# Layer 0 transposed on TensorE for all chunks, and another order of the weight loads, in a four-layer attention and feed-forward kernel

## The chip, the core and the metric

The kernel runs on one core of a Trainium2 chip. The metric is the device time of one execution in microseconds (us); lower is better. Times of runs are given with their median. The profile is that of one execution. Its names for the engines are PE (TensorE), PEld (TensorE's loads of the stationary operand), DVE (VectorE), ACT (ScalarE), POOL (GpSimd) and SP (SyncE, which here issues DMAs only). DMAs are issued on two queues, that of SP and that of ACT, and are carried out by 16 DMA engines.

## The reference

Four residual layers follow one another on x of 2048 rows (tokens) by 448 columns, in bf16: attention, feed-forward, attention, feed-forward. Both attention layers use the same weights, and so do both feed-forward layers.

```python
def _A_ref(x, wqkv, wo):                 # H = 16 heads of Dh = 28, window W = 8, dilation 2
    q, k, v = ...                        # x @ wqkv, split into heads
    idx = pos[:, None] - off[None, :]    # off = 0, 2, ..., 14; only idx >= 0 counts
    logits = jnp.einsum("bhsd,bhswd->bhsw", q, kg) * scale
    attn = _softmax(logits, axis=-1)
    o = jnp.einsum("bhsw,bhswd->bhsd", attn, vg)
    return o... @ wo

def _B_ref(x, w_gate, w_up, w_down):     # F = 1792
    h = (x @ w_gate) * (x @ w_up)
    return h @ w_down

x = x + _A_ref(_layernorm(x), A_wqkv, A_wo)
x = x + _B_ref(_layernorm(x), B_w_gate, B_w_up, B_w_down)
x = x + _A_ref(_layernorm(x), A_wqkv, A_wo)
x = x + _B_ref(_layernorm(x), B_w_gate, B_w_up, B_w_down)
```

## The kernel before

**Tiling.** Even tokens and odd tokens are put into the two halves of a 2048-column order, so that a dilated window becomes a window of 8 neighbours. Everything is cut along the tokens: 16 blocks of 128 for the normalisation, chunks of 256 or 512 (`ACH`, `BCH`, line 56) for the projections, and 17 query blocks of 120 or 128 for the attention. A job such as A03 is chunk 3 of layer 0, B10 is chunk 0 of layer 1. `SEQ` (line 65) lists the 19 jobs. All of x stays in SBUF (`x_sb`), and all weights are loaded once.

**A job of attention.** `ln_chunk` (line 570) normalises each block: statistics on DVE (line 580), the inverse root on ACT (lines 583 and 585), the normalised block `xn_sb` on DVE (line 601). The block then has to be transposed into `xnTa`. `PE_T` (line 28) lists the chunks for which TensorE does it: four transposes into one bank of PSUM (line 610), and one copy to `xnTa` on ACT or DVE (line 616). All other blocks go through one DMA transpose each, issued by SP (line 604). Layer 0 has the chunks 00 to 04 with 2, 4, 4, 4 and 2 blocks. `qk_chunk` (line 668) multiplies with the query and key weights (matmuls recorded at line 648), and ACT or DVE copies the result to `qk` (line 700). The last 4 heads' values of most query blocks take another path: their weights are packed into unused columns of the query/key projection (line 531), SP writes these rows of the result to a tensor `vt` in HBM (line 709), and a DMA transpose brings them back as columns of `v2_sb` (line 720; the profile calls the destination `v_sb`). The rows of ones that go with them are written to `vt` by SP once (line 540). Then follow the scores (line 791), the exponential (ACT, line 798), the mask (DVE or POOL, line 804), the product with the values (line 824; with ones at line 818 for the first four query blocks), the division, and the product with `wo` (line 664), which is added to `x_sb` (line 876).

**A job of feed-forward.** The normalised block is transposed by DMA into `xnTb`. Fourteen units of 14 matmuls (line 905) make gate and up from `WGU`, whose partitions 0 to 63 hold the gate weights and 64 to 127 the up weights. ACT copies the gate (line 911), DVE multiplies (line 914). The result times `WD` (lines 664 and 926) is added to `x_sb`.

**What sets the order.** A planner in the file (`Sched`, line 112) fixes the order of all instructions on each engine before the program is built. It simulates the engines with an assumed duration for each operation and an assumed latency (`lat`) for each DMA, and at each step lets a free engine take the ready operation with the lowest priority number. For TensorE it also weighs changes of the matmul's tile mode (`HOLD_A`, `HOLD_BA`, `HOLD_BB`). Priorities come from the job's place in `SEQ`, a table by job (`JP`), one by kind of operation (`PR`), and for layer 0's normalisation `HEAD_P`. On the chip each engine runs its list in order and waits on semaphores where an operation needs another's result. A wrong assumption thus leaves the order in place and turns into a wait.

**The loads around the change.** SP issues x, part of the query/key/value weights, `wo` (line 544), and the up weights (line 545) without any wait but for the memset of `wo_g`. ACT issues the gate weights (line 546) when the first key projection is complete, and the down weights in two halves (line 548) when the first eight blocks are normalised and the first part of chunk 01's projection is copied out. `BL` (line 53) holds the assumed latencies of gate, up and down weights.

Of the kernel before, what the change touches and what calls it, by code (L numbers as in the profile page):

```python
# [24 lines left out]
ACT_TABLE_SET = 6  # L25

MAIN = "R64"
PE_T = ('00', '01', '02')
HEAD_LN = 5
HEAD_P = (-38.93, -34.69, -18.9, -18.15, -15.19)  # L30
HOLD_A = 0.0
HOLD_BA = 2000.0
HOLD_BB = 2000.0
HOLD_N = 3
D_PE = 1
# [9 lines left out]
AVC = True  # L45
AVC_E = ("act", "dve")
NBK = 8
PR = {'E': 5.39, 'lnv': 4.48, 'N': 2.54, 'S': 1.51, 'H': -16.8, 'VT': 0.06, 'QK': 1.71, 'G': -2.51, 'R': -2.54, 'Tps': 24.4, 'Ddps': -3.29, 'V': 4.0, 'Yps': -16.04, 'rstd': -2.61, 'Rs': -4.21, 'Rl': -7.93, 'mv': -22.02, 'Ex': 2.02, 'Oc': 6.51, 'QKps': -1.79, 'x': -0.68, 'Gps': 21.63, 'PW': -1.17, 'bn': 1.13, 'xn': 0.26, 'T': -5.31, 'AV': 2.17, 'VVps': -0.71}
JP = {'A04': 17.51, 'B32': 73.91, 'B33': -39.49, 'A00': -57.97, 'B12': -8.89, 'A22': 3.6, 'B10': -7.69, 'B14': -6.07, 'B13': -6.69, 'A21': -6.5, 'B11': 5.61, 'B31': 5.7, 'B34': -23.55, 'A01': -1.05, 'A23': -9.97, 'A02': -0.45, 'A20': -23.59, 'B30': 0.59, 'A03': -0.27}
XL = (3000.0, 3000.0, 4500.0, 5000.0, 5500.0)  # L50
WVL = 5000.0
STL = (3300.0, 4300.0, 3500.0, 4600.0)
BL = (9000.0, 13000.0, 11000.0)
WOL = 6000.0
PLAIN = 4
ACH = {0: (256, 512, 512, 512, 256), 2: (512, 512, 512, 512)}
BCH = {1: (256, 512, 512, 512, 256), 3: (256, 512, 512, 512, 256)}
WARM = 18
FILL = 30
SEED = 459  # L60
JITTER = 0
ATT_P = 0.26
A_CAP = 5
B_CAP = 8
SEQ = "A00 A01 B10 A02 B11 A03 A04 B12 A20 B13 A21 B14 B30 A22 B31 A23 B32 B33 B34".split()
# [28 lines left out]

class Op:
    __slots__ = ("engs", "ins", "est", "deps", "mode", "prio", "acquire", "release", "idx", "eng",
                 "dma", "lat", "after", "start", "end", "seen", "selfd")

    def __init__(self, **kw):
        for k in self.__slots__:  # L100
# [11 lines left out]
class Sched:  # L112
# [10 lines left out]
        self.ready = {}  # L123
        self.rng = random.Random(SEED)

    def add(self, engs, ins, est, deps=(), prio=0.0, mode=None, acquire=None, release=(), dma=None, lat=0.0, after=None, selfd=()):
        if isinstance(engs, str):
            engs = (engs,)
        if not isinstance(est, dict):
            est = {e: float(est) for e in engs}  # L130
        op = Op(engs=engs, ins=ins, est=est, deps=[d for d in deps if d is not None], mode=mode, prio=prio,
                acquire=acquire, release=release, idx=len(self.ops), dma=dma, lat=lat, after=after, selfd=set(selfd))
        op.deps += list(selfd)
        op.prio += JITTER * self.rng.random()
        for _, k in ins:
            k = k[0] if isinstance(k, list) and k else k
            if isinstance(k, tuple) and k[0] in PR and k[0] != "cross":
                op.prio += PR[k[0]]
                break
        self.ops.append(op)  # L140
        for n, (fn, keys) in enumerate(ins):
            for k in (keys if isinstance(keys, list) else [keys]):
                if k is not None:
                    assert k not in self.ready, k
                    self.ready[k] = (op, n)
        return op
# [11 lines left out]
    def ready_at(self, op, eng):  # L158
        r = 0.0
        for k in op.deps:  # L160
            f = self.finish_of(k)
            if f is None:
                return None
            src = self.ready[k][0]
            if src.dma is not None:
                lat = 60.0
            elif src.eng == eng:
                lat = (self.SELF_LAT if k in op.selfd else 0.0) if eng == "pe" else self.SAME + self.TAIL[eng]
            else:
                lat = self.PE_LAT if src.eng == "pe" else self.LAT + self.TAIL[src.eng]  # L170
            r = max(r, f + lat)
        if op.after is not None:
            if op.after.end is None:
                return None
            r = max(r, op.after.end)
        return r
# [18 lines left out]
    def schedule(self):  # L195
# [27 lines left out]
        while left:  # L223
            moved = False
            b_ready = any(o.acquire is not None and o.acquire.kind == 1 for o in pend["pe"])
            for e in self.ENGS:
# [54 lines left out]
                if op.acquire is not None:  # L281
                    op.acquire.b = self.pick_banks(op.acquire, now)
                    for b in op.acquire.b:
                        self.holder[b] = op.acquire
                        if self.last_rel[b] is not None:
                            op.deps.append(self.last_rel[b])
                est = op.est[e]
                if e == "pe":
                    if mode is not None and op.mode != mode:
# [115 lines left out]
def build(nc, A_x, A_wqkv, A_wo, B_w_gate, B_w_up, B_w_down, out):  # L405
# [41 lines left out]
    sc = Sched()  # L447
    LAST = sc
    sem_names = ["pe", "act", "dve", "pool"]
    sem_names += [f"d_x{i}" for i in range(NCH)] + ["d_stg0", "d_stg1", "d_stg2", "d_stg3", "d_wv", "d_wo", "d_wg", "d_wu", "d_wd0", "d_wd1", "d_out", "d_out2"]  # L450
    sem_names += ["d_x0h"]
    sem_names += [f"d_t{li}_{j}" for li in range(4) for j in range(len(CH[li]))]
    sem_names += [f"d_p{li}_{j}" for li in (0, 2) for j in range(len(CH[li]))] + [f"d_v{q}" for q in range(NQB)] + ["d_one0", "d_one2", "d_stv"]
# [6 lines left out]
        atl = mybir.InstLoadActFuncSet(name=nc.get_next_instruction_name(), ins=[], outs=[], act_func_set_id=ACT_TABLE_SET)  # L460
        return E.add_instruction(atl)

    def plain_dma(q, dst, src, key, sem, deps=(), lat=3000.0, prio=0.0):
        sc.add(q, one(lambda E: E.dma_start(dst, src), key), {"sp": 520.0, "act": 500.0, "pool": 1000.0}[q], deps=deps, dma=sem, mode=0, lat=lat, prio=prio)  # L464

    CH_ROWS = [0, 128, 192, 320]
    stage = hT[:].rearrange("p f s n -> p (f s n)")
# [69 lines left out]
    sc.add("pool", one(lambda E: E.memset(big1, 1.0), "c_big1"), 1800, prio=-20)  # L537
    for li in (0, 2):
        dst = vt_dram[li].rearrange("(t r) n -> t r n", r=32)[:, DH:32, :]
        plain_dma("sp", dst, big1, ("vones", li), f"d_one{li}", deps=["c_big1"], lat=3000.0, prio=-30)  # L540
    for j in range(4):
        dst = wo_g[32 * j:32 * j + DH, :, :]
        src = A_wo.rearrange("(c j e) d -> j e c d", c=4, j=4, e=DH)[j]
        plain_dma("sp", dst, src, ("wo", j), "d_wo", deps=["c_wo"], lat=WOL, prio=-45)
    plain_dma("sp", WGU[64:128, :, :], B_w_up.rearrange("(k p) f -> p k f", p=64), "wu", "d_wu", lat=BL[1], prio=-44)
    plain_dma("act", WGU[0:64, :, :], B_w_gate.rearrange("(k p) f -> p k f", p=64), "wg", "d_wg", lat=BL[0], deps=[("Kps", 0, 0, 0)], prio=-90)
    for n in range(2):
        plain_dma("act", WD[:, 7 * n:7 * n + 7, :], B_w_down[F // 2 * n:F // 2 * n + F // 2, :].rearrange("(c p) e -> p c e", p=128), ("wd", n), f"d_wd{n}", deps=[("rstd", 0, 7), ("QK", 0, 1, 0)], lat=BL[2], prio=-19)
    WDR = [("wd", 0), ("wd", 1)]
    WO = [("wo", j) for j in range(4)]  # L550

# [18 lines left out]
    def ln_chunk(li, j, prio):  # L570
# [17 lines left out]
        for B in blocks:  # L588
# [13 lines left out]
                   325.0 if par == 0 else 540.0, deps=[("rstd", li, B), ("mv", li, B), ("x", li - 1, B), prev], prio=prio - 0.2)  # L602
            if not by_pe:
                sc.add("sp", one(lambda E, slot=slot, c0=c0: E.dma_start_transpose(X[:, :, c0:c0 + 128], xn_sb[:, slot, 0:128 * nt]), ("T", li, B)),
                       1300.0, deps=[("xn", li, B)] + war, dma=f"d_t{li}_{j}", mode=0, lat=3000.0 if li == 0 else 1400.0 if par == 0 else 1900.0, prio=prio)
            else:
                bk = Banks(1)
                ins = []
                for c in range(4):
                    ins.append((lambda E, c=c, slot=slot, bk=bk: E.transpose(ps[:, bk[0], :].bitcast(bf)[:, 128 * c:128 * (c + 1)], xn_sb[:, slot, 128 * c:128 * (c + 1)], ident[:]),  # L610
                                ("Tps", li, B) if c == 3 else None))
                sc.add("pe", ins, 4 * 56.0, deps=[("xn", li, B), "c_id"], mode="F", acquire=bk, prio=prio)
                def ft(E, c0=c0, bk=bk):
                    src = ps[:, bk[0], :].bitcast(bf)[:, 0:512].rearrange("p (c n) -> p c n", c=4)
                    dst = X[:, :, c0:c0 + 128]
                    return E.activation(dst, src, ACT.Copy) if hasattr(E, "activation") else E.tensor_copy(dst, src)
                sc.add(("act", "dve"), one(ft, ("T", li, B)), {"act": act_est(512), "dve": dve_est(512)}, deps=[("Tps", li, B)] + war, release=[(bk, 0)], prio=prio)
# [50 lines left out]
    def qk_chunk(li, j, prio):  # L668
# [37 lines left out]
        for b, w in [(b, w) for b in range(4) for w in range(2) if b + w < 4 and (li, j) != (0, 0)]:  # L706
            src = qk[32 * b + DH:32 * b + 32, w, :, c0:c1]
            dst = vt_dram[li].rearrange("(t w b r) n -> r w b t n", w=2, b=4, r=4)[:, w, b, :, c0:c1]
            sc.add("sp", one(lambda E, dst=dst, src=src: E.dma_start(dst, src), ("PW", li, j) if b == 3 else None), 550.0, deps=[("QK", li, j, c) for c in range(4)], dma=f"d_p{li}_{j}", mode=0, lat=3500.0 if li == 0 and j <= 2 else 2200.0, prio=prio - 0.2)

    vslot, v2slot = {}, {}

    def vt_load(li, qb, prio):
# [3 lines left out]
        slot, prev = ring("v2", ("AV", li, qb))  # L717
        v2slot[(li, qb)] = slot
        deps = [("PW", li, j) for j in chunks_of(li, k0, k0 + nk)] + [("vones", li), prev]
        sc.add("sp", one(lambda E: E.dma_start_transpose(v2_sb[:, slot, :], vt_dram[li][:, k0:k0 + 128]), ("VT", li, qb)), 1300.0, deps=deps, dma=f"d_v{qb}", mode=li, lat=2500.0 if li == 0 and k0 < 1024 else 1500.0, prio=prio)  # L720

    def v_group(li, qbs, prio):
        X = xnT[0]
# [161 lines left out]
    def b_chunk(li, j, n_b, prio):  # L885
# [7 lines left out]
        def unit(fc):  # L893
            acq = Banks(2, kind=1)
            def out(which):
                return ps[:, acq[which], 0:nt]
            return dict(bk=acq, out=out, n=nt, deps=["wg", "wu"],
                        keys=(("Gps", li, j, fc), ("Ups", li, j, fc)), fc=fc)

        us = [unit(fc) for fc in range(FC)]  # L900
# [158 lines left out]
```

## Time and profile before

Thirteen runs took 398.99 to 405.2 us, with a median of 404.39 us.

| | value |
|---|---|
| profiled execution, device time | 404.39 us |
| its span, from the first to the last instruction | 402.7 us |
| matmuls | 5046 |
| HBM read / written | 8.54 MB / 2.83 MB |
| transposes by TensorE (line 610) | 40, from 7.6 to 19.6 us |
| DMA transposes into `xnTa` in layer 0 (line 604) | 6, issued from 25.1 to 38.2 us |
| first feed-forward matmul (line 905) | 59.78 us |
| last matmul (line 926) begins a group at | 394.77 us |

A row of the views by engine reads: line, engine, operation, output tile <- input tiles, the shape, the number of instructions behind an x. What stands in brackets is idle time of that engine before the row, and what ended it. In the timeline a row begins with its start and its length in us, and neighbours of one kind are merged. In the page's 40 slices one digit stands for a fortieth of the span, about 10 us, and gives the busy share in tenths. In a view of windows a row gives the stretch, its length, and for PE, PEld, DVE, ACT and POOL the busy us and the number of instructions, then the granted TensorE clock as a share of the full one, the share of the DMA engines' time and GB/s. A view of waits gives the waiting engine and line, what ended the wait, the sum in us, how often, and the longest.

### The profile page before, as it was taken

To read this page: it belongs to the slowest core of one execution; us is meant where nothing else is said; L and a number is where in the kernel's file an instruction comes from. 1 tells how busy PE (TensorE), PEld (TensorE's weight loads), DVE (VectorE), ACT (ScalarE), POOL (GpSimd) and SP (SyncE) were. 2 spreads that over 40 slices of the span, in tenths; PEclk is the share of its full clock that TensorE was granted. 3 is DMA by queue.
4 is the path that set the end of the run, shared out by engine and by line. 5 is a ranking of instruction groups with operands and counts; after the bars stand their busy time and mean duration, and the time that the engine had idled before them with its cause. 6 is when DMAs were issued, how large, how long until landed. Compare 5 with 4: busy or idle time off the path is not lost.

```text
span 402.7 us, 11719 instructions
## 1 busy us (share of the span) xinstructions
PE 387.9 (96%) x5046; PEld 210.5 (52%) x5046; DVE 293.3 (73%) x603; ACT 223.4 (55%) x406; POOL 15.4 (4%) x28
## 2 busy tenths in 40 slices
PE   8994999999999999999999999999999999999996
PEld 5541457644454444545455676744445455444584
DVE  5986498989997988688688955936684777674152
ACT  5874487666753945565564565624661575343040
POOL 6223000000000000000000000000000000000000
PEclk9998799999999999999999999999999999999999
DMA  8999141325025112222020205031030300320010
GB/s 267 239 240 197 25 61 27 62 54 67 12 47 73 29 30 45 47 28 39 15 40 10 54 13 105 18 60 43 11 47 24 70 0 3 91 48 2 13 36 24
DMA packets 57171, 23.34 MB, mean 58 GB/s; under 512 B 48064, under 2 KB 56192, under 8 KB 57120
## 3 DMA queue, kind: packets, MB, share of 16 engines
q1 hardware_dynamic: 54400, 18.86, 24.4%
q10 hardware_dynamic: 2720, 3.73, 3.9%
q8 instruction: 40, 0.66, 0.6%
q14 instruction: 11, 0.09, 0.1%
HBM read 8.54 MB, written 2.83 MB: 28 GB/s over the span
## 4 chain that ended last, share of the span: by engine, by line
PE 86%; DVE 4%; DMA 4%; ACT 3%; issue 1%; SPq 0%; DVEq 0%
PE ps L905 42%; PE ps L664 26%; PE ps L648 13%; DMA xnTa<-xn_sb 3%; PE ps L824 2%; PE ps L791 2%; DMA x_sb<-in_A_x_dram 1%; ACT E_sb L798 1%; PE ps L926 1%; DVE E_sb L804 1%; ACT qk L700 1%; DVE x_sb L876 1%; DVE xn_sb L601 0%; SPq L464 0%; DVE qk L700 0%
## 5 line engine op out<-in xcount | busy, mean ns | idle before, releaser
L905 PE MATMUL ps<-xnTb,WGU 64*128 64x512 bf16 (+1 forms) x1960 | 179.3, 333 | 2.2 <-DVE R_sb L840 0.8
L905 PEld LDWEIGHTS ps<-xnTb,WGU 64*128 64x128 bf16 x1960 | 96.3, 94 | 73.7 <-issue 2.2
L911 ACT ACTIVATE g_sb<-ps 128x512 bf16<-128x512 f32 (+1 forms) x140 | 71.4, 512 | 89.1 <-PE ps L905 88.0
L914 DVE TENSOR_TENSOR hT<-g_sb,ps 128x512 bf16<-128x512 bf16 (+1 forms) x140 | 78.9, 573 | 45.3 <-ACT g_sb L911 42.5
L664 PE MATMUL ps<-WD,hT 64*128 64x448 bf16 x840 | 85.3, 349 | 0.2
L798 ACT ACTIVATE E_sb<-ps 128x960 bf16<-128x960 f32 (+1 forms) x68 | 62.6, 972 | 11.2 <-PE ps L791 11.1
L648 PE MATMUL ps<-xnTa,WQK 64*128 64x512 bf16 (+1 forms) x504 | 55.2, 360 | 6.6 <-DMA xnTa<-xn_sb 6.0
L664 PEld LDWEIGHTS ps<-WD,hT 64*128 64x128 bf16 x840 | 39.8, 94 | 37.1 <-PE ps L664 1.1
L876 DVE TENSOR_TENSOR x_sb<-x_sb,ps 128x448 bf16<-128x448 bf16 x62 | 35.9, 613 | 16.0 <-PE ps L664 15.7
L804 DVE TENSOR_TENSOR E_sb<-E_sb,MK 128x960 bf16<-128x960 bf16 (+1 forms) x64 | 43.8, 699 | 4.5 <-ACT E_sb L798 4.5
L580 DVE BATCH_NORM_STATS2 st<-x_sb 128x6 f32<-128x448 bf16 x64 | 37.4, 613 | 3.0 <-DMA x_sb<-in_A_x_dram 3.0
L648 PEld LDWEIGHTS ps<-xnTa,WQK 64*128 64x128 bf16 x504 | 23.4, 95 | 30.6 <-issue 8.3
L601 DVE TENSOR_SCALAR xn_sb<-x_sb,mv,rstd 128x512 bf16<-128x512 bf16 (+1 forms) x64 | 34.3, 569 | 1.0 <-ACT rstd L585 0.8
L664 PE MATMUL ps<-wo_g,oT 64*128 64x448 bf16 x256 | 29.6, 350 | 0.0
L700 ACT ACTIVATE qk<-ps 128x1024 bf16<-128x1024 f32 (+1 forms) x22 | 19.7, 906 | 17.1 <-PE ps L648 17.1
L700 DVE CAST qk<-ps 128x1024 bf16<-128x1024 f32 (+1 forms) x14 | 16.0, 1142 | 12.0 <-PE ps L648 12.0
L842 ACT ACTIVATE R_sb<-R_sb 128x480 f32<-128x480 f32 (+1 forms) x30 | 18.0, 603 | 10.4 <-DVE R_sb L840 10.2
L648 PE MATMUL ps<-WV,xnTa 64*128 64x336 bf16 (+2 forms) x252 | 22.8, 301 | 0.1
L858 DVE TENSOR_TENSOR oT<-O_sb,R_sb 128x480 bf16<-128x480 f32 (+3 forms) x32 | 19.5, 614 | 2.6 <-ACT R_sb L844 2.5
L844 ACT ACTIVATE R_sb<-R_sb 128x480 f32<-128x480 f32 (+1 forms) x34 | 20.3, 602 | 0.6
L840 DVE STREAM_SHUFFLE R_sb<-O_sb 128x480 f32<-128x480 f32 (+1 forms) x30 | 20.5, 689 | 0.0
L583 ACT ACTIVATE lnv<-mv,eps_sb 128x2 f32<-128x2 f32 (+1 forms) x33 | 9.7, 293 | 18.1 <-DVE mv L582 17.9
(55 smaller groups left out, 179.4 us busy)
## 6 DMA issues: line engine op xcount, KB each, us to landing
out_dram<-x_sb SPq DMA_DIRECT2D x15, 112.0 KB, 1.7
WGU<-in_B_w_up_dram SPq DMA_DIRECT2D x1, 1568.0 KB, 17.6
WGU<-in_B_w_gate_dram ACTq DMA_DIRECT2D x1, 1568.0 KB, 20.3
WD<-in_B_w_down_dram ACTq DMA_DIRECT2D x2, 784.0 KB, 15.9
x_sb<-in_A_x_dram SPq DMA_DIRECT2D x3, 448.0 KB, 5.8
vt<-qk SPq DMA_DIRECT2D x49, 16.0 KB
xnTb<-xn_sb SPq DMA_TRANSPOSE x32, 3.0
v_sb<-vt SPq DMA_TRANSPOSE x30, 2.7
```

The source lines that it names most:

```text
L580: sc.add("dve", one(lambda E, B=B: E.bn_stats(st6[:, B, :], x_sb[:, B, :]), ("bn", li, B)), 525.0, deps=[("x", li - 1, B)] + ([("xn", li - ...
L601: sc.add("dve", one(lambda E, B=B, dst=dst, src=src: E.tensor_scalar(dst, src, mv[:, B, 0:1], rstd[:, B:B + 1], ALU.subtract, ALU.mult), ( ...
L648: parts[0 if s < 3 else 1][1].append((lambda E, w=w, c=c, lo=lo, st=st, sp_=sp_: E.matmul(u["out"](w), u["lhs"](w, c, lo, lo + 64), u["rhs ...
L664: ins.append((lambda E, w=w, c=c, lo=lo, st=st, sp_=sp_: E.matmul(outs(w), lhs(w, c, lo), rhs(w, c, lo), start=st, stop=sp_), keys[w] if s ...
L700: return E.activation(dst, src, ACT.Copy) if hasattr(E, "activation") else E.tensor_copy(dst, src)
L798: return E.activation(E_sb[0:nk, slot, 2 * hp:2 * hp + 2, 0:4 * nq], ps[0:nk, b0:b0 + 2, 0:4 * nq], ACT.Exp, scale=SCALE)
L804: return E.tensor_tensor(e, e, m, ALU.mult)
L840: sc.add("dve", one(lambda E: E.stream_shuffle(R_sb[:, rs, 0:4 * nq], osrc(), [DH] * 32), ("Rs", li, qb)), dve_est(4 * nq) + 100.0, deps=[ ...
L876: sc.add("dve", one(lambda E: E.tensor_tensor(x_sb[:, B, :], x_sb[:, B, :], ps[:, bk[w], 0:D], ALU.add), ("x", li, B)), dve_est(D), deps=[ ...
L905: ins.append((lambda E, u=u, k=k, w=w: E.matmul(u["out"](w), WGU[64 * w:64 * w + 64, k, 128 * u["fc"]:128 * u["fc"] + 128], X[64 * w:64 * ...
L911: sc.add("act", one(lambda E, gs=gs, bk=bk: E.activation(g_sb[:, gs, 0:nt], ps[:, bk[0], 0:nt], ACT.Copy), ("G", li, j, fc)), act_est(nt), ...
L914: sc.add("dve", one(lambda E, gs=gs, bk=bk, fc=fc: E.tensor_tensor(hT[:, fc, hs, 0:nt], g_sb[:, gs, 0:nt], ps[:, bk[1], 0:nt], ALU.mult), ...
```

## The change

All five chunks of layer 0 are transposed on TensorE. The down weights are issued by SP, before the up weights, without a wait. The gate weights (ACT) and the up weights (SP) are each cut into two pieces, of 3 and 4 of the 7 parts of `WGU`, each with a semaphore of its own, and the feed-forward matmuls wait for all four. In place of its wait, a gate piece gets an earliest time in the planner's own simulation (`tmin`, from `KT`: 13.0 and 13.5 us). The planner adds a dependency for such an operation if SP issues it. The rows of ones for `vt` get a later priority. The assumed latencies change, and so do all priority tables, one hold time, the number `ATT_P` and the seed.

```diff
-PE_T = ('00', '01', '02')
+PE_T = ("00", "01", "02", "03", "04")
-HEAD_P = (-38.93, -34.69, -18.9, -18.15, -15.19)
-HOLD_A = 0.0
-HOLD_BA = 2000.0
+HEAD_P = (-41.16, -25.35, -17.52, -19.02, -16.79)
+HOLD_A = 2000.0
+HOLD_BA = 4000.0
...
-BL = (9000.0, 13000.0, 11000.0)
+BL = (11000.0, 15000.0, 8000.0)
+KP = ((0, 3), (3, 7))
+KT = (13000.0, 13500.0)
...
-ATT_P = 0.26
+ATT_P = -0.3
...
+        if op.tmin is not None:
+            r = max(r, op.tmin)
...
+                if op.tmin is not None and e == "sp":
+                    gate = [o for o in order["pe"] if o.end + self.PE_LAT <= now and isinstance(o.ins[-1][1], tuple) and o.ins[-1][1] in self.ready]
+                    op.deps.append(gate[-1].ins[-1][1])
...
-        plain_dma("sp", dst, big1, ("vones", li), f"d_one{li}", deps=["c_big1"], lat=3000.0, prio=-30)
+        plain_dma("sp", dst, big1, ("vones", li), f"d_one{li}", deps=["c_big1"], lat=3000.0, prio=-10)
...
-    plain_dma("sp", WGU[64:128, :, :], B_w_up.rearrange("(k p) f -> p k f", p=64), "wu", "d_wu", lat=BL[1], prio=-44)
-    plain_dma("act", WGU[0:64, :, :], B_w_gate.rearrange("(k p) f -> p k f", p=64), "wg", "d_wg", lat=BL[0], deps=[("Kps", 0, 0, 0)], prio=-90)
+    for n, (k0, k1) in enumerate(KP):
+        plain_dma("sp", WGU[64:128, k0:k1, :], B_w_up[64 * k0:64 * k1, :].rearrange("(k p) f -> p k f", p=64), ("wu", n), f"d_wu{n}", lat=BL[1], prio=-43.5)
+        plain_dma("act", WGU[0:64, k0:k1, :], B_w_gate[64 * k0:64 * k1, :].rearrange("(k p) f -> p k f", p=64), ("wg", n), f"d_wg{n}", lat=BL[0], tmin=KT[n], prio=-90)
     for n in range(2):
-        plain_dma("act", WD[...], ..., ("wd", n), f"d_wd{n}", deps=[("rstd", 0, 7), ("QK", 0, 1, 0)], lat=BL[2], prio=-19)
+        plain_dma("sp", WD[...], ..., ("wd", n), f"d_wd{n}", lat=BL[2], prio=-44)
...
-            return dict(bk=acq, out=out, n=nt, deps=["wg", "wu"],
+            return dict(bk=acq, out=out, n=nt, deps=[(w, n) for w in ("wg", "wu") for n in range(2)],
```

Also changed, in numbers only: the tables `PR` and `JP`, `SEED`, and three more assumed DMA latencies (layer 0's transposes, writes of `vt` and transposes back).

## The prediction

> **What bounds the kernel now.** I read the page first, for the shares and the 40 slices:
>
> ```profile
> PE 387.9 (96%) x5046; PEld 210.5 (52%) x5046; DVE 293.3 (73%) x603; ACT 223.4 (55%) x406; POOL 15.4 (4%) x28
> PE   8994999999999999999999999999999999999996
> PEclk9998799999999999999999999999999999999999
> DMA  8999141325025112222020205031030300320010
> ```
>
> TensorE is busy for 387.9 of 402.7 us, so 14.8 us are all that a better order can win without shortening its work. Two slices stand out, the fourth and fifth (10 us each, 30 to 50 us): there the busy digit is 4 and the granted clock dips. Next I asked what TensorE itself waited for, longest first:
>
> ```profile
> PE ps L648 <- DMA xnTa<-xn_sb: 6.0, 1, 6.0
> PE ps L515 <- DVE eps_sb L493: 1.1, 1, 1.1
> PE ps L926 <- DVE hT L914: 0.9, 1, 0.9
> PE ps L905 <- DVE R_sb L840: 0.8, 1, 0.8
> ```
>
> One wait holds 6 of the 14.8 us: a query/key projection waits for a normalised block that the DMA transposes. Nothing else passes 1.1 us, and from 60 to 390 us the idle time sums to 1.7 us (from windows of 40, 100, 100 and 90 us). The timeline of TensorE and of the SP queue shows the place:
>
> ```profile
> 32.92 1.69 PE L648 MATMUL ps<-xnTa,WQK 64*128 64x512 bf16 x14
> 40.65 1.46 PE L648 MATMUL ps<-xnTa,WQK 64*128 64x512 bf16 x6 [6.04 <-DMA xnTa<-xn_sb]
> 42.04 0.59 PE L818 MATMUL ps<-E_sb,ones 128*32 128x480 bf16 x4
> ...
> 25.11 6.95 SPq L604 DMA_TRANSPOSE xnTa<-xn_sb  x4
> 32.11 3.02 SPq L709 DMA_DIRECT2D vt<-qk  x7
> 35.17 4.36 SPq L604 DMA_TRANSPOSE xnTa<-xn_sb  x2
> ```
>
> The four transposes of chunk 03 are issued from 25.11 us; the last lands at 40.5 us. The chain of waits agrees: it contains one piece of 10.62 us, from 29.90 us, for such a transfer. Layer 0's six transposes land a median 9.5 us after issue, layer 2's sixteen 2.5 us. The difference is the traffic beside them: the gate and up weights (1568 KB each, issued at 11.38 and 10.25 us, landing 20.3 and 17.6 us later), then the two halves of the down weights (issued at 21.46 and 22.09 us, 14.7 to 17.1 us to land). The plan in the kernel priced the transposes at 3.0 us, so its order of TensorE is 6.5 us too optimistic there: that is the stall.
>
> The windows show what the stall costs afterwards:
>
> ```profile
> 34.60:40.65 6.05, 0.01 (x3) 0.03 (x1) 2.85 (x3) 0.27 (x1) 1.99 (x1) 0.80 1.19 140
> 40.65:45.80 5.15, 5.15 (x42) 1.72 (x42) 0.66 (x1) 2.05 (x3) 0.00 (x0) 0.57 0.06 10
> 45.80:50.00 4.20, 4.20 (x64) 2.30 (x62) 3.40 (x5) 2.05 (x4) 0.00 (x0) 1.00 0.12 23
> ```
>
> The seventh value is the granted clock (0.57 for 5.15 us after the stall), the eighth the DMA share.
>
> **What the Trainium skill says.** "TensorE: Matmul & The Clock Gate", Part 1: an idle window of about 3.4 us drops TensorE to half its clock, and about 3.4 us of work bring it back. The trace agrees (0.57 on average for 5.15 us, then 1.00). Part 4 of that page prices a 128x128 TensorE transpose at about 275 ns in a kernel, output to PSUM, so with a copy after it. Here one lasts 219 ns, but they overlap: four cost less than half of four durations. "DMA: Bandwidth & Descriptors", Queues, rings and completion order: each DMA engine consumes one issuer's ring in order and alternates between issuers by packet. So SP's transposes shared the engines with ACT's weights, which the 9.5 us against 2.5 fit; it also says that what SP issues behind big weights on its own queue starts behind them. No wait of this trace isolates that.
>
> **The change part by part.**
>
> 1. *The stall goes*: the six DMA transposes of chunks 03 and 04 become TensorE transposes. −6.04 us of idle time.
>
> 2. *The clock after it*: between 40.65 and 45.80 us TensorE did 22 projections of 512 columns (6 + 16), one set of 4 ones-matmuls and one of 16 value products. At full clock 28 such projections took 3.12 us (21.56 to 24.68 us), so 22 take 2.45; the two sets took 0.56 (21.00 to 21.56 us). 3.01 us against 5.15: −2.14 us. If a shorter stall of over 3.4 us stays, this part stays too.
>
> 3. *Transposes on TensorE*: 6 blocks x 4 = 24. Starts in the timeline: eight take 0.55 us (13.67 to 14.22), four 0.33 us (14.77 to 15.10), so 69 to 83 ns each: 1.7 to 2.0 us on the engine that bounds. I take +2.0.
>
> 4. *Their copies out of PSUM*: 6 more, of 0.60 us on ACT or 0.39 on DVE, 2.4 to 3.6 us in all. From 25 to 35 us ACT is busy 8.80 of 10 us, DVE 7.61: 3.6 us free together, a thin cover; from 34.6 to 50 us both are half empty. I take 0, upper bound 3.6. A bank of PSUM is held for each; same bound. A gain here is excluded, it is added work.
>
> 5. *Queues.* SP loses six transpose issues (6.95 + 4.36 = 11.3 us of its time) and gains the two halves of the down weights and one more up piece, three at 0.39 to 0.76 us: +1.2 to 2.3 us near 10 us. Behind these on SP stand the constant rows of `vt` (11.06 us now), which move back too by their own priority, then the `vt<-qk` writes, the transposes into `v_sb`/`v2_sb`, and those into xnTb. First `vt<-qk` today waits until 32.11 us, behind the transposes, though its last input is copied out at 27.34 us; it can now be issued some 4.8 us earlier. ACT loses two issues (0.77 us at 21.5 us) and gains one of 0.39 to 0.69 us near 13 us. The 13.0/13.5 us release is used only by the planner: its extra dependency is written for SP, and the gate pieces are issued by ACT, so no wait is added. Sum on the path: 0, between −0.5 and +0.5.
>
> 6. *When the weights land.* Ahead of them come x (1.84 MB), wqkv (1.2) and wo (0.4). By 10 us 2.67 MB are moved (182 and 351 GB/s for 5 us each); the remaining 0.8 MB and 3 x 1.61 MB at the 243 GB/s of 10 to 35 us need 23 us: all is in at about 33 us, at the 209 GB/s of the slowest window at 37 us. The gate and up weights, last instead of first, come 2 to 5 us later than their 31.7 us; their first user starts at 59.78 us, 8 us earlier if the stall goes: 51.6 us. The cover is 15 us. The down weights are used at 76.6 us. Cost 0.
>
> 7. *New priorities everywhere, another tie order*: the order of all engines is planned anew. Between 60 and 390 us at most 1.7 us of idle can be won, some 1.8 more at the start of the second chunk and the end (0.84 + 0.93). It can also lose: I bound it by −2.5 and +4 (twice as much idle again as that part and the two small waits have). I take 0.
>
> Sum: −6.04 − 2.14 + 2.0 = −6.2 us against the profiled execution, 404.39 us with a span of 402.7. That execution equals the median of the 13 runs. **398.2 us.** The fastest run of the kernel before, 398.99 us, is near what remains if the stall is almost absent, which fits.
>
> **The rivals.**
>
> *The wait moves (part of the gain is kept or none).* Without the stall ACT and DVE must do the work of 25 to 50 us in 17; the copies of point 4 (3.6) or a worse order (4) come onto the path: 398.2 + 3.6 to 398.2 + 7.6, 402 to 406. For it: ACT and DVE are 88% and 76% busy there. Against it: through the stall they idle, so the work left over is small.
>
> *The values come late: slower than before.* Value products from the fifth query block on need columns that go out by `vt<-qk` and return transposed, all on SP. On SP's queue the down and up weights are now ahead of them. By point 6 these end at 33 to 37 us; the writes take 2 us more, the transpose 1.3 to issue and 2.7 to land: 39 to 43 us. Today the fifth product stands at 57.45 us, moved up by 8.2 it is at 49 us, and there is no wait. It decides if the new order puts that product before about 40 us. The fourth block's scores are at 32.60 us, so 33 us is the earliest that I can argue: 10 us of wait to 43 and 2.1 us for the clock, 398.2 + 12.1 = 410.3 us. Gate and up weights used before 33 to 37 us would do the same, but the first feed-forward chunk needs attention output, normalisation and transposes first, 13.5 us today (46.33 to 59.78).
>
> *The change doesn't do what it says.* If the pipeline of copies had bounded 35 to 50 us anyway, removing the DMA wait would bring nothing and the transposes cost 2: 406.4 us. Against it: ACT was idle 7.8 us before its next step in the stall, DVE 6.5 us.
>
> **How the numbers follow.** A measurement of this kernel can tell about 1% from no change: 400.35 and 408.43 us are the limits. The stall goes and nothing takes its place: 0.64, 395 to 400.3. The wait moves, or nothing is won: 0.22, 400.4 to 408. Late values, late weights or a clearly worse order: 0.14, over 408.4. The low end is 398.2 − 2.5 (point 7) − 0.3 (point 3) − 0.5 (point 5), about 394.9, with 0.4 for a run's own spread: 394.5. The high end, 406.0, takes in the first rival's bound (405.8); about 0.06 lies below, and 0.14 above. Faster 0.64, same 0.22, slower 0.14.
>
> **What would show it.** Right: no wait of TensorE for xnTa in layer 0, a granted clock of 1.00 from 5 us on, 64 TensorE transposes instead of 40, first feed-forward product near 52 us. Point 4 wrong: TensorE waits for ACT or DVE copies between 15 and 50 us. Point 5 or 6 wrong: a wait of TensorE for `v_sb<-vt`, WGU or WD. Point 7 wrong: more than 3 us of idle between 60 and 390 us. The forecast falls if a wait over 3.4 us, with the clock after it, stands anywhere else.

## The result, and the profile after

The kernel after takes **399.75 us** (median of 11 runs, 398.79 to 400.33); beside it the kernel before takes 404.06 us (48 runs, 398.99 to 405.7). The ratio is 0.9915, with a 95% interval of 0.9887 to 0.9943. The ratio leaves out runs of a kernel that are more than 1.5% above its fastest, ten of the 48 of the kernel before, so it stands nearer to 1 than the quotient of the medians (0.9893). The forecast was 398.2 us within 394.5 to 406. The profiled execution took 398.79 us with a span of 397.1, against 404.39 and 402.7: 5.6 us less. It is the fastest of the 11 runs, and the profiled execution before lies at the median of its own, so the traces show a larger gain than the 4.3 us between the medians.

The page of the kernel after, shares and slices:

```profile
PE 386.9 (97%) x5070; PEld 212.7 (54%) x5070; DVE 289.6 (73%) x599; ACT 227.2 (57%) x413; POOL 16.2 (4%) x31
PE   8988999999999999999999999999999999999996
PEclk9999999999999999999999999999999999999999
DMA  8992142412212310221120224203103020320000
```

The hole in the fourth slice and the dip of the clock in the fourth and fifth are gone, and the DMA engines are full for three slices, not four. But the third and fourth slice show an 8 for TensorE. The waits of TensorE in the kernel after, longest first:

```profile
PE ps L522 <- DVE eps_sb L500: 1.1, 1, 1.1
PE ps L934 <- DVE hT L922: 0.9, 1, 0.9
PE ps L656 <- DVE oT L866: 0.8, 1, 0.8
PE ps L913 <- DMA xnTb<-xn_sb: 0.8, 1, 0.8
PE ps L618 <- DVE qk L708: 0.7, 1, 0.7
PE ps L656 <- ACT WQK L530: 0.5, 1, 0.5
PE ps L826 <- DVE E_sb L812: 0.5, 1, 0.5
PE ps L618 <- DVE xn_sb L609: 0.5, 1, 0.5
```

(Line numbers are 7 or 8 higher than before.) No wait for a transposed block of layer 0 is left. In its place stand four short ones for VectorE between 22 and 35 us, 0.7 + 0.5 + 0.5 + 0.8 = 2.5 us.

The books by stretch, from windows of TensorE's busy time, before and after:

```profile
0.00:60.00 60.00, 50.30 (x675) 27.50 (x677) 43.69 (x95) 39.76 (x72) 15.35 (x28) 0.94 0.81 173
0.00:60.00 60.00, 54.99 (x778) 32.96 (x780) 49.15 (x108) 45.47 (x86) 16.24 (x31) 1.00 0.65 164
```

From 0 to 60 us it idled 9.70 us before and 5.01 us after, so 4.7 us are won there. From 60 to 380 us it is 1.74 against 1.83 us, no change. Busy time over the whole span fell by 1.0 us although 24 transposes were added, because work at a lower clock counts as busy for longer.

### The profile page after: what moved, and what is told of

Same layout as the page of the kernel before. It is cut to its first block, busy times and chain, and to the rows that moved or that the text cites. A ratio compares the mean times of both kernels' runs of the same rounds, so it can differ in the third digit from the quotient of the medians.

```text
span 397.1 us, 11796 instructions
## 1 busy us (share of the span) xinstructions
PE 386.9 (97%) x5070; PEld 212.7 (54%) x5070; DVE 289.6 (73%) x599; ACT 227.2 (57%) x413; POOL 16.2 (4%) x31
## 3 DMA queue, kind: packets, MB, share of 16 engines
q10 hardware_dynamic: 912, 2.12, 2.0%
## 4 chain that ended last, share of the span: by engine, by line
PE 84%; DVE 9%; DMA 3%; SPq 1%; issue 1%; ACT 1%; DVEq 0%
PE ps L913 42%; PE ps L672 25%; PE ps L656 12%; PE ps L799 2%; PE ps L832 2%; DVE xn_sb L609 2%; DVE st L588 2%; DMA x_sb<-in_A_x_dram 2%; DVE E_sb L812 2%; PE ps L934 1%; SPq L471 1%; DMA xnTb<-xn_sb 1%; DVE qk L708 1%; DVE x_sb L884 1%; DVE hT L922 0%
## 5 line engine op out<-in xcount | busy, mean ns | idle before, releaser
L656 PE MATMUL ps<-xnTa,WQK 64*128 64x512 bf16 (+1 forms) x504 | 53.0, 353 | 0.8 <-ACT WQK L530 0.5
L812 DVE TENSOR_TENSOR E_sb<-E_sb,MK 128x960 bf16<-128x960 bf16 (+1 forms) x64 | 42.6, 673 | 4.2 <-ACT E_sb L806 4.2
L609 DVE TENSOR_SCALAR xn_sb<-x_sb,mv,rstd 128x512 bf16<-128x512 bf16 (+1 forms) x64 | 36.2, 601 | 1.3 <-ACT rstd L593 1.2
L708 ACT ACTIVATE qk<-ps 128x1024 bf16<-128x1024 f32 (+1 forms) x28 | 25.2, 916 | 14.2 <-PE ps L656 13.9
L672 PEld LDWEIGHTS ps<-wo_g,oT 64*128 64x128 bf16 x256 | 12.4, 94 | 11.4 <-DVE x_sb L884 0.3
L656 PEld LDWEIGHTS ps<-WV,xnTa 64*128 64x128 bf16 x252 | 11.6, 94 | 10.5 <-ACT R_sb L852 1.2
## 6 DMA issues: line engine op xcount, KB each, us to landing
WGU<-in_B_w_up_dram SPq DMA_DIRECT2D x1, 896.0 KB, 19.2
```

The source lines that it names most:

```text
L609: sc.add("dve", one(lambda E, B=B, dst=dst, src=src: E.tensor_scalar(dst, src, mv[:, B, 0:1], rstd[:, B:B + 1], ALU.subtract, ALU.mult), ( ...
L656: parts[0 if s < 3 else 1][1].append((lambda E, w=w, c=c, lo=lo, st=st, sp_=sp_: E.matmul(u["out"](w), u["lhs"](w, c, lo, lo + 64), u["rhs ...
L672: ins.append((lambda E, w=w, c=c, lo=lo, st=st, sp_=sp_: E.matmul(outs(w), lhs(w, c, lo), rhs(w, c, lo), start=st, stop=sp_), keys[w] if s ...
L812: return E.tensor_tensor(e, e, m, ALU.mult)
```

## The experiments

All variants but one keep the planned order of every engine (*frozen*): the plan is made as usual, and the lists are edited after `sc.schedule()`. So a part of the change can be done or undone without a new plan. The runs fall into three groups on three chips. The kernel before ran beside each group, and its median moved between 402.34 and 403.29 us, so differences of half a microsecond between groups say little. The second number under "runs" counts those whose granted clock, averaged over the whole run, lies below 1.00.

| run | what it is | runs, below 1.00 | median us | before beside it | ratio, 95% interval |
|---|---|---|---|---|---|
| b_weights | before, only the weight loads changed | 6, 6 | 405.87 | 402.34 | 1.0102 [1.0063, 1.0141] |
| b_fill | before, the wait filled with idle matmuls | 20, 0 | 400.88 | 402.34 | 0.9979 [0.9958, 1.0001] |
| a_oldw | after, weight loads of before | 20, 0 | 400.29 | 402.34 | 0.9953 [0.9937, 0.9969] |
| a_look | after, unchanged | 4, 0 | 399.73 | 403.29 | 0.9897 [0.9861, 0.9933] |
| a_dma6 | after, six DMA transposes again | 5, 2 | 400.01 | 403.29 | 0.9903 [0.9870, 0.9936] |
| a_dma6l | the same, issued later | 5, 4 | 400.29 | 403.29 | 0.9916 [0.9886, 0.9947] |
| a_dma2 | the same, chunk 04 alone | 4, 0 | 399.78 | 403.29 | 0.9901 [0.9866, 0.9936] |
| a_dma6o | after, both structural parts undone | 20, 11 | 400.34 | 402.54 | 0.9969 [0.9945, 0.9992] |
| b_pet | before, TensorE transposes, planned anew | 4, 3 | 407.93 | 402.54 | 1.0151 [1.0082, 1.0219] |
| a_nopool | after, POOL's four masks on VectorE | 12, 0 | 398.54 | 402.54 | 0.9910 [0.9878, 0.9941] |
| a_npd | a_nopool with a_dma6l | 4, 0 | 397.62 | 402.54 | 0.9897 [0.9822, 0.9971] |

**The kernel before, once more (b_look).** No edit.

> The kernel before, unchanged, looked at once more. My reading: its time moves between 399 and 405.7 us with the length of the one wait of TensorE for xnTa in layer 0. Then a look at 403 to 405 us shows that wait at 4 to 6 us with the clock dip behind it, and a look near 399 to 400 us shows it under 3 us without a dip. The rival, that the spread comes from elsewhere: the wait is 6 us whatever the time.

402.55 us. The timeline of TensorE in this execution:

```profile
39.10 0.88 PE L648 MATMUL ps<-xnTa,WQK 64*128 64x512 bf16 x6 [4.54 <-DMA xnTa<-xn_sb]
39.91 0.59 PE L818 MATMUL ps<-E_sb,ones 128*32 128x480 bf16 x4
...
44.32 0.93 PE L664 MATMUL ps<-wo_g,oT 64*128 64x448 bf16 x8
```

The wait is 4.54 us where it was 6.04, and from its end to the first `wo` product (line 664) 5.22 us pass where it was 5.68 (40.65 to 46.33). Together 1.96 us less; the time is 1.84 us less. So this pair of executions differs by that one wait and its clock.

The other runs of the kernel before carry only the granted clock of the whole run, 0.992 in the first profiled execution and 0.996 in this one. Beside the experiments there are 81 of them: 6 at 1.00 took 398.2 to 398.9 us, 40 at 0.995 or 0.996 took 399.6 to 403.8 us, and 35 at 0.991 or 0.992 took 402.2 to 405.9 us. So the time goes with the clock that was lost, as one wait of changing length would have it, though no trace of a run near 399 us shows the wait itself. In its best executions the kernel before is thus about 1 us faster than the median of the kernel after, as far as groups can be compared. The change takes away a loss that most executions have, not all.

**The clock alone (b_fill).** Forty matmuls on a zeroed operand ahead of the waiting projection:

```diff
+    n = next(n for n, o in enumerate(sc.order["pe"]) if ("T", 0, 13) in o.deps)
+    q = sc.order["pe"][n]
+    b = q.acquire.b[0]
+    f = Op(engs=("pe",), ins=[(lambda E: E.matmul(ps[:, b, 0:256], warm[:, 0:128], warm, start=True, stop=True), None)] * 40, ...)
...
+    sc.order["pe"].insert(n, f)
```

> Kernel before, order frozen, with 40 extra matmuls of 256 columns on a zeroed operand put into TensorE's list just ahead of the projection that waits (some 4.3 us, inside the 6.0 us of waiting). They compute nothing that is used. My theory: the wait's second part, 2.1 us at a lower clock, goes, and nothing else: 402 us (401.5 to 402.5), with a granted clock of 1.00 from 34 to 46 us. Rival (the work after the stall is paced by copies, so the clock costs nothing): 404 us within 0.5. If the wait is often shorter than 4.3 us, the extra matmuls cost time in those runs.

```profile
34.56 4.54 PE L1010 MATMUL ps<-hT 128*128 128x256 bf16 x40
39.03 0.82 PE L648 MATMUL ps<-xnTa,WQK 64*128 64x512 bf16 x6
39.79 0.39 PE L818 MATMUL ps<-E_sb,ones 128*32 128x480 bf16 x4
...
42.67 0.93 PE L664 MATMUL ps<-wo_g,oT 64*128 64x448 bf16 x8
```

400.88 us. The projection starts no later than in b_look, and the same work up to the `wo` product now takes 3.64 us (39.03 to 42.67) in place of 5.22 and 5.68: the clock's price was 1.6 and 2.0 us. The granted clock is 1.00 over the whole of all 20 runs. The medians differ by 1.5 us, where 2.1 were expected, and the ratio's interval just includes 1, so the gain in time is not clear of noise. The filling also has a price: in this execution the last transpose of chunk 03 landed at 36.55 us, so without the extra matmuls the wait would have been 2 us, and they held the projection up. That fits the times: all but one of the 20 runs lie within 400.4 and 401.5 us, neither as slow as most runs of the kernel before nor as fast as its best.

**The weight loads alone (b_weights).** The pieces of the gate weights keep the wait of before.

```diff
+    wd = [sc.order["act"].pop(pos("act", ("wd", n))) for n in range(2)]
+    for o in wd:
+        o.eng, o.deps = "sp", []
+    n = pos("sp", "wu")
+    sc.order["sp"][n:n + 1] = wd + [dma_op("sp", *up(0, 3), "wu", "d_wu"), dma_op("sp", *up(3, 7), "wu2", "d_wu")]
...
+    sc.order["act"][n:n + 1] = [dma_op("act", *gate(0, 3), "wg", "d_wg", [("Kps", 0, 0, 0)]), dma_op("act", *gate(3, 7), "wg2", "d_wg")]
```

> Kernel before with its order of all engines frozen; only the weight loads are those of the change (down ahead of up on SP, gate and up in two pieces). Chunk 03 and 04 still go by DMA transpose. My theory (the transposes on TensorE make the gain, since a DMA transpose cannot pass the weights): the transposes stand behind the weights on SP, the wait of TensorE stays at 4 us or more, 402 to 406 us. Rival (the order of the weights alone makes the gain: they are all in before the transposes matter): the wait falls to 1 us or less and the dip goes, 395.5 to 398 us.

405.87 us, slower. Its longest wait (6.7 of the 7.2 us are in layer 0), and the SP queue's timeline:

```profile
PE ps L648 <- DMA xnTa<-xn_sb: 7.2, 2, 6.7
...
25.16 12.51 SPq L604 DMA_TRANSPOSE xnTa<-xn_sb  x4
37.71 4.60 SPq L709 DMA_DIRECT2D vt<-qk  x7
```

The four issues take 12.51 us in place of 6.95, and the slowest transpose lands after 14.7 us in place of 10.7. With more weights ahead on their own queue the transposes are issued and land later still, and none of the six runs is under 405.08 us. The order of the weights does nothing good by itself.

**The weight loads undone (a_oldw).** The reverse edit on the kernel after.

> Kernel after with its order frozen; only the weight loads are those of before (up first on SP in one piece, gate in one piece on ACT when the first key projection is done, the two halves of down on ACT once block 7 is normalised and the first part of chunk 01 is copied). All transposes of layer 0 stay on TensorE. My theory: the weights' order costs and brings nothing once no DMA transpose is beside it: 399.7 us within 0.7. Rival (the weights' order carries the gain): 402 us or more, with a wait of TensorE for WGU, WD or the values that come back from HBM.

400.29 us, within the 0.7 us that were expected, and no wait for weights. Against the 399.73 and 399.75 us of the kernel after, measured in other groups, the weights' order is worth some half a microsecond at most.

**The transposes undone on the new order (a_dma6, a_dma6l, a_dma2).** The TensorE transposes and their copies are taken out of the lists, and a DMA transpose is put into SP's for each (here as in a_dma6):

```diff
+        sc.order["pe"].remove(tp)
+        sc.order[ft.eng].remove(ft)
...
+        o.ins = one(lambda E, B=B, slot=slot: E.dma_start_transpose(xnT[0][:, :, 128 * B:128 * B + 128], xn_sb[:, slot, 0:512]), ("T", 0, B))
...
+    n = next(n for n, o in enumerate(sc.order["sp"]) if o.dma == "d_p0_1")
+    sc.order["sp"][n:n] = [moved[B] for B in [10, 11, 12, 13, 14, 15] if B in [10, 11, 12, 13]]
```

> Kernel after with its order frozen, but the six blocks of chunks 03 and 04 transposed by DMA again; four of the six are issued by SP ahead of the first writes of vt (near 25 us, while weights are still in flight), two behind them. Their 24 matmuls and six copies are left out. My theory: the transposes stand behind the weights and hold up SP, so the projection of chunk 03 and the first values that come back from HBM are late: 403 to 407 us, with waits of TensorE for xnTa or v_sb. Rival (with the new order the transposes on TensorE are needless): the weights are in by 31 us and the projection starts near 40 us, so no wait, and 24 matmuls of 69 to 83 ns are saved: 397.5 to 398.2 us.

> The same, but all six DMA transposes stand behind the first writes of vt on SP, from 27.4 us on. My theory, sharpened by the run that moved only the weights: it is the overlap with the weights that makes these transposes slow, not the DMA path; here most of them run after 31 us, with the weights in, so they land by 38 us, before the projection's start near 40 us: 397.5 to 398.5 us, 1.5 to 2 us less than after. Rival (SP's queue is now too full: the transposes back of the values are issued 7 us later, near 42 us, and are late for the product at 43.9 us): 400.5 to 402 us.

> The same for the two blocks of chunk 04 alone, behind the first writes of vt. Its projection starts at 53 us, so nothing waits; 8 transposes and two copies are saved: 0.6 to 0.7 us less than after, 399.1 us. If the price of a transpose on TensorE is hidden, no change.

400.01, 400.29 and 399.78 us beside 399.73: neither the loss nor the gain that was expected. The waits of TensorE in a_dma6, and the place of the one for `xnTa`:

```profile
PE ps L656 <- DVE oT L866: 1.4, 1, 1.4
PE ps L618 <- DVE qk L708: 1.3, 1, 1.3
...
PE ps L656 <- DMA xnTa<-xn_sb: 1.1, 1, 1.1
...
PE ps L826 <- DVE E_sb L812: 0.9, 1, 0.9
...
256.90 5.36 PE L656 MATMUL ps<-xnTa,WQK 64*128 64x512 bf16 x48 [1.05 <-DMA xnTa<-xn_sb]
```

The transposes stand behind the weights here too (from the first of four issues to the end of the last 14.17 us pass). But the last of chunk 03 lands at 35.7 us, and the projection that needs it has its place near 41 us, so TensorE does not wait for `xnTa` in layer 0 at all; the 1.1 us are a wait in layer 2. And the waits for VectorE grew by 1.6 us (0.8 to 1.4, 0.7 to 1.3, 0.5 to 0.9): TensorE, relieved of some 2 us of work, waited longer for VectorE. So the 24 transposes lay in time that TensorE would otherwise have waited.

They seem to keep the clock up as well. Four of the five runs of a_dma6l and two of those of a_dma6 have a clock below 1.00. In the trace of a_dma6l:

```profile
22.00:24.30 2.30, 0.57 (x6) 0.23 (x4) 2.30 (x5) 0.78 (x2) 2.12 (x1) 1.00 1.03 276
24.30:27.70 3.40, 3.37 (x36) 1.94 (x38) 2.75 (x8) 1.82 (x5) 0.00 (x0) 0.50 1.07 329
```

Without the eight transposes that stand at 22.16 us in the kernel after, two waits of 1.3 and 0.5 us lie close together, with 0.4 us of work between them, and then the clock is at half for 3.4 us, although no wait of this trace is longer than 1.4 us. The work from 24.33 to 28.35 us takes 4.02 us, and 2.73 in the trace of a_dma6, where the same two waits left the clock at 1.00: some 1.3 us lost.

**Both structural parts undone (a_dma6o).** The edits of a_dma6 and a_oldw together; only the new plan is left.

> Kernel after with its order frozen and both other parts of the change undone: six DMA transposes for chunks 03 and 04 (four ahead of the first writes of vt, two behind) and the weight loads of before. What is left of the change is the new plan. Theory now (after moving the weights alone cost 2 to 4 us on the old order, and putting the DMA transposes back on the new order cost nothing): the new plan is what removes the wait, since its projection of chunk 03 starts near 40 us instead of 34.6: 399.5 to 401.5 us. Rival (the two structural parts each do half: either one is enough, both undone bring the wait back): 402.5 to 405 us, with a wait of TensorE for xnTa of 3 us or more.

400.34 us, and no wait for `xnTa` in layer 0 (0.4 us in layer 2). So the new order avoids the long wait without either part, if narrowly: the last transpose of chunk 03 lands at 40.4 us, less than 1 us ahead of the first projection that needs it. It does not give all of the gain. Eleven of the 20 runs have a clock below 1.00, and they spread from 398.96 to 402.39 us, where the kernel after stays within 398.79 and 400.33. Beside the kernel before it is 0.3% faster by the ratio, the kernel after 0.85 to 1.0%; by the medians 2.2 us against 3.6 to 4.3. The profiled execution is one of those at 1.00, so what lowers the clock in the others stays open.

**TensorE's transposes with the old priorities (b_pet).**

```diff
-PE_T = ('00', '01', '02')
+PE_T = ('00', '01', '02', '03', '04')
...
-HOLD_BA = 2000.0
+HOLD_BA = 4000.0
```

> Kernel before with chunks 03 and 04 transposed by TensorE, planned anew with the old priorities and the old weight loads. Without a second change the planner finds no order, so one hold time is that of the change (4.0 instead of 2.0 us). Theory (without DMA transposes no wait over 3.4 us is left, whatever the plan): 398 to 401.5 us, clock 1.00 throughout. Rival (the old priorities carry the loss): 402 us or more.

407.93 us: the theory missed, and the rival's range holds. (The change itself sets two hold times, `HOLD_A` and `HOLD_BA`; only the second is taken over here.) The wait for `xnTa` in layer 0 is gone, and the first feed-forward product starts at 57.69 us, 2.1 us earlier. But a new plan is a new plan for all four layers, and this one loses elsewhere. Its longest waits:

```profile
PE ps L905 <- DMA xnTb<-xn_sb: 2.9, 1, 2.9
PE ps L664 <- DVE oT L858: 1.8, 1, 1.8
```

The first is at 353.69 us: from 350 to 380 us TensorE is busy for 27.09 us in place of 30.00. The second is in layer 0, before 38.01 us. From 60 to 380 us it idles 6.58 us in place of 1.74. The total therefore says nothing of the transposes; it shows how much a plan weighs. It doesn't isolate them in layer 0 either, since this plan too asks for chunk 03 later, near 45 us.

**VectorE beside POOL (a_nopool, a_npd).** Why does the new order wait for VectorE? In the kernel after, VectorE is busy for 9.78 of the 10 us from 20 to 30. Its timeline and POOL's:

```profile
18.34 2.55 DVE L609 TENSOR_SCALAR xn_sb<-x_sb,mv,rstd 128x512 bf16<-128x512 bf16 x2
18.62 2.12 POOL L812 TENSOR_TENSOR E_sb<-E_sb,MK 128x1024 bf16<-128x1024 bf16 x1 [4.76 <-ACT rstd L593]
...
28.39 2.22 POOL L812 TENSOR_TENSOR E_sb<-E_sb,MK 128x960 bf16<-128x960 bf16 x1 [4.21 <-ACT E_sb L806]
29.00 2.12 DVE L812 TENSOR_TENSOR E_sb<-E_sb,MK 128x960 bf16<-128x960 bf16 x1
```

Two normalisations that take 0.7 us elsewhere take 2.55, a mask of 0.65 us takes 2.12: each ends just after the POOL mask beside it. The edit gives POOL's masks to VectorE:

```diff
+    for qb in range(NQB):
+        o = sc.ready[("E", 0, qb, 1)][0]
+        if o.eng == "pool":
+            sc.order["pool"].remove(o)
+            o.eng = "dve"
+            sc.order["dve"].insert(pos("dve", ("E", 0, qb, 0)) + 1, o)
```

> Kernel after with its order frozen; the four masks that POOL does (some 2.1 us each) are done by VectorE instead, right behind the other half's mask. Theory: from 13 to 35 us VectorE sets the pace of the new kernel, and beside a POOL mask its operations on SBUF stretch (0.69 us of two normalisations to 2.55, a mask of 0.65 to 2.12, three normalisations from 1.03 to 1.51), 3.8 us in all; the four masks cost VectorE 2.6 us. So TensorE's waits of 20 to 35 us (2.5 us) shrink by 1 to 2 us: 398 to 399 us. Rival (the stretched operations are not what TensorE waits for, and VectorE only gets more work): 399.7 us or up to 1 us more.

> The same, and the six DMA transposes behind the first writes of vt as in the earlier run. Theory: taking the 24 transposes off TensorE brought nothing because TensorE then waited longer for VectorE; with VectorE freed it brings up to 2 us more: 396.5 to 398.5 us. Rival (something else paces this stretch): the same as with the masks moved alone, within 0.5.

398.54 and 397.62 us. VectorE's timeline in a_npd:

```profile
18.86 0.70 DVE L609 TENSOR_SCALAR xn_sb<-x_sb,mv,rstd 128x512 bf16<-128x512 bf16 x2
...
26.88 3.00 DVE L812 TENSOR_TENSOR E_sb<-E_sb,MK 128x960 bf16<-128x960 bf16 x5 [0.20 <-ACT E_sb L806]
```

The stretching is gone; five masks take 3.00 us. In the trace of a_nopool TensorE idles 4.04 us up to 60 us, against 5.01 in the kernel after and 4.76 in a_look: less work on POOL and more on VectorE wins 0.7 to 1.0 us there. The medians differ by 1.2 us (398.54 against 399.73 and 399.75), but these come from other groups, and the intervals of the ratios overlap, so the size is not sure. With the transposes taken off TensorE as well the median falls by another 0.9 us. That rests on four runs, 396.64 to 398.32 us, against 397.46 to 399.03 for a_nopool: likely, not shown. a_npd has the lowest median of all kernels here.

## Why the prediction was right, and where its reason was not

*Time and range.* 399.75 us lies in the range, 1.55 us above the 398.2 of the sum. By the medians the change is 1.07% faster, by the ratio 0.85%, so it lies on the border that the prediction drew at 1% between "faster" (0.64) and "the same" (0.22).

*Points 1 and 2, the stall and the clock.* Right in kind and size: the wait is absent from the trace after, and b_fill and b_look put the clock's share at 1.6 to 2.0 us for waits of 4.5 and 6.0 us; 2.14 was forecast. Two readings were loose. Only the fourth slice shows a 4; the fifth shows a 9, since slow matmuls count as busy. And 398.99 us, the fastest run before, does not fit an absent stall: by the prediction's own sum the kernel before without it, and without the 2.0 us of new transposes, would take 396.2 us, so some 2.8 us of loss were left in that run.

*Why the stall goes* was misjudged. The prediction put it down to the transposes on TensorE alone. On the new order TensorE does not wait for DMA transposes in layer 0 either (a_dma6, a_dma6l, a_dma6o). What changed is also when the order calls for the blocks: the first projection of chunk 03 has its place at 34.6 us before and near 40 us after, within this row of the trace after:

```profile
39.46 2.32 PE L656 MATMUL ps<-xnTa,WQK 64*128 64x512 bf16 x20
```

The DMA transposes of chunk 03 had all landed at 40.5 us before, and at 35.7 to 40.4 us in those three runs. The prediction gave the new plan 0 in point 7 and did not ask whether the plan by itself would avoid the wait. From 60 us on, the 0 was right. That the sum came out near the measured time is thus in part luck: the plan, set at nothing, avoids the wait on its own and brings new short waits that were not in the sum.

The transposes on TensorE still have a part in the gain. On the new order none of the 40 runs of a_oldw, a_look, a_dma2 (all chunks but 04 on TensorE) and a_nopool has a clock below 1.00, and none of the kernel after; 17 of the 30 runs of a_dma6, a_dma6l and a_dma6o have. (In a_npd, without POOL's masks, none of four has.) Whether they would have removed the stall on the old order was not run. In the trace before, the fourth block of chunk 03 is normalised by 29.90 us, when its DMA transpose is issued, 4.7 us before the order asks for it. So they may well have been enough there too, which is an estimate.

*Points 3 and 4, transposes and copies.* The sum charged 2.0 us on TensorE and let VectorE and ACT be covered. On the new order it is the other way round: the transposes fill gaps (removing them gains nothing, a_dma6), and TensorE waits for VectorE from 20 to 35 us, 2.5 us of short waits. This is the first rival in a small version. A part of the reason, POOL's masks holding up VectorE, was in the trace before, unnoticed beside the large wait:

```profile
32.15 2.01 POOL L804 TENSOR_TENSOR E_sb<-E_sb,MK 128x960 bf16<-128x960 bf16 x1 [9.01 <-ACT E_sb L798]
32.37 2.30 DVE L804 TENSOR_TENSOR E_sb<-E_sb,MK 128x960 bf16<-128x960 bf16 x1
```

*Points 5 and 6, queues and weights.* The first write of `vt` is issued at 24.89 us, 7.2 us earlier (4.8 were forecast); the last piece of the weights, of up, lands at 33.4 us (14.23 + 19.2), and 33 to 37 were forecast. The weights took SP 5.0 us of issuing (9.84 to 14.83 us) where it was 0.76, more than the 1.2 to 2.3 us of the forecast, but nothing that TensorE waited for stood behind them. The second rival, values that come late, stayed away, but by less than forecast: the fifth query block's product stands at 43.88 us, not 49, and its transposes are issued from 35.03 us.

*A detail that missed:* the first feed-forward product was to start near 52 us, and starts at 56.01. That line left out the 2.0 us of transposes that the sum itself charges. Beyond these TensorE idles some 1.3 us more than the forecast allows, and does some 1.2 us more of layer 0's work ahead of the product (estimates from its busy time up to there). Such a mark, set for a plan that is not the old one, says little.

*What stays open:* how long the wait is in the fastest runs of the kernel before; what TensorE's transposes would do on its frozen order; what lowers the clock in half of the runs of a_dma6o; and whether the old priorities with TensorE's transposes would be as good under a plan as well tuned as the new one.

## What to carry to other kernels

In a statically ordered kernel a wait belongs to a pair: a result that is late and an order that asks for it. Before crediting the mechanism that makes the result earlier, freeze the order and undo that mechanism alone. If nothing is lost, the mechanism was not needed under the new order; that does not say that it would not have been enough under the old one. Compare the spread of the runs as well as the medians: here the order alone avoids the long wait, but with DMA transposes on it 17 of 30 runs lost clock, and with those on TensorE none of 40. And count TensorE's waits with its clock: one of 6.0 us cost 2.0 us more. It is not only the single wait that counts: in the kernel after four short ones spread over 13 us, 2.5 us together, left the clock at 1.00, while in a_dma6l two close together, 1.8 us, were followed by 3.4 us at half clock (and the same two in a_dma6 were not).

## What the runs showed of the hardware that was not expected

A POOL mask holds up some of VectorE's operations on SBUF: two normalisations and a mask lasted until just after it (2.55 in place of 0.70 us, 2.12 in place of 0.65). Others kept their time beside one: a copy from PSUM at 22.25 us took its usual 1.21 us, and in the trace before two statistics at 21.17 us, which read one operand from SBUF, took 1.14 us, as they do at 41.86 us after with POOL idle. The Trainium skill has this on the page "SBUF — State Buffer", Who interferes with whom: the two share a pair of ports, which a VectorE instruction needs if it reads two operands from SBUF or runs in a mode that uses two ports, and whoever issues first holds the pair for the whole instruction. The trace agrees. A POOL mask of 2.1 us thus took up to 1.9 us of VectorE's time to spare it one of 0.65 us.

Four DMA transposes issued behind weights on the same queue took SP 12.5 us (b_weights) and 14.2 us (a_dma6) to issue, a single one up to 6.3 us, where one takes some 1.3 us with the weights in. Whatever SP issues next waits for that.
